# A chunk-attention and Fourier-mixing kernel: who issues the lower tiles' stores, and the order of the work around the first group's down projection

## The chip, the cores and the metric

The kernel runs on one core of one Trainium2 chip. The core has a matrix engine (TensorE, PE in the profile, with its weight loads shown as PEld), a vector engine (VectorE, DVE), a scalar engine (ScalarE, ACT), a general-purpose engine (GpSimd, POOL) and a sync engine (SyncE, SP) that only issues DMAs. Each engine has its own list of instructions and takes them in order; they meet through semaphores. The metric is the device time of one execution in microseconds (us).

## The reference

Eight batches of 576 tokens, 8 heads of 64. Attention runs within chunks of 64 tokens; the heads are joined to 512 features; then a Fourier mix and a two-layer network follow, with 2048 hidden features.

```python
scores = scale * np.matmul(q_c, k_c.transpose(0, 1, 2, 4, 3))      # chunks of 64
attn = softmax(scores)
x = (attn @ v_c) -> (B, S, H*D)
mixed = np.real(fft(fft(x, axis=1), axis=2))
u = x + mixed
un = (u - mean(u)) / sqrt(var(u) + 1e-6)
out = u + relu(un @ w_ch1) @ w_ch2
```

## The kernel before, in words

**Tiles and groups.** Tokens are taken in tiles of 128: per batch two *lower* tiles (`LO`, chunks from the front), two *higher* tiles (`HI`, chunks from the back, kept in mirrored order), and per pair of batches one *remainder* tile (`RE`). Group g of the two-layer network (g = 0 to 7) is the four tiles of batch g, in the order LO, HI, LO, HI; group 8 is the four remainder tiles. `first[b]` is the number of batch b's first tile; where b is even, that is its remainder tile.

**One main loop.** `mlp(g)` is a generator that emits the matrix work of group g: an up phase and a down phase. Each of its `yield`s is one step t of the main loop at the end of the kernel; in a step the loop emits, behind that matrix work, a share of everything else: the attention and Fourier work of the next batch (`side(b)`, a generator too), the rounding of weights, the sums and stores described below, and fetches. Nothing reorders this: what is emitted first stands first in its engine's list. Group 0's up phase is t = 1 to 16, its down phase (`down_plain`, L1236 and L1249) t = 17 to 32, where `begin[1]` = 32. `side(1)` is spread so that it ends at `ready_at[0]` = 25; its last three parts are the calls of `mixed` (L838 to L855), one for the remainder tile and two for the pairs of LO and HI tiles. They run the second Fourier product into a PSUM tile of tag `pt` (two buffers), copy half of it out on ACT (L843), join the halves on DVE (L848, L849), add them to the tile (on DVE for LO, on POOL for HI, L855) and take mean and variance (L702 to L707).

**Between two groups.** `normed(g, s)` normalises tile s (for g = 1 on ACT, L990 to L992), `turned(g, s)` transposes it on PE (L397) and copies it to `unT` (L1007). `combined(g, q)` makes sums of `unT`'s quarters on DVE (L1024 to L1028). Group 0's down phase calls `normed(1, j)` after block m = 9 + j and `turned(1, j)` after m = 11 + j, and `combined` right behind `turned` for j = 2 and 3.

**Fast products.** Groups 1 to 7 multiply with seven products in place of eight (`up_halves`, L1289; `down_halves`, L1341), which needs sums of the weights' quarters. For the first weight, `keep1(pair)` (four POOL instructions, L1069) makes three sums and overwrites one quarter, for one of four pairs of column blocks. Group 1 reads these sums in place; from group 2 on they, and the raw quarters, come back from a DRAM table `s1` through ten slabs (`fetch(1)`, L1155). `keep1_store` (L1074) writes the seven parts of each pair to `s1`, 256 KB each, 28 in all. For the second weight `keep2` (L1087, L1091) and `keep2_whole` (L1099) do the same into `s2`, read through three slabs of 1 MB (`fetch(2)`, L1160). `keep1(0)` is emitted at t = 31, pairs 1 to 3 at t = 33, 35, 37; the 28 stores two per step from t = 33. `conv2` runs the four `keep2` three parts per step, once all weights are rounded.

**Weights.** They arrive as 8-byte numbers, 512 KB a piece (L346), and are rounded to 4 bytes by a chain of DVE and ACT instructions (`round_weight`, L362 to L386).

**Stores of the result.** `store(n, o)` writes a finished tile: a lower tile as two DMAs of 64 rows in reversed order (L1037), both on SP; a higher tile as four DMAs, two on SP and two on ACT (L1046). SP also issues every load of q, k, v (L250, L273) and every fetch.

The lines in the loop that matter:

```python
ready_at = [begin[g] + (2 * KF - 7 if g < first_of[2] else 2 * HF + 4) for g in range(NG)]
conv2 = iter([step for i in range(HF // 2) for step in [keep2(i ^ 1)]])
...
if begin[1] - 1 <= t < begin[1] + 7 and t % 2:
    keep1((t - begin[1] + 1) // 2)
```

Of the kernel before, what the change touches and what calls it, by code (L numbers as in the profile page):

```python
# [16 lines left out]
def kernel(  # L17
# [32 lines left out]
    nc = tc.nc  # L50
# [350 lines left out]
    def att_T(n, which="qk"):  # L401

        if n > first[2]:
            for src, dst, nm in ((qs, qT, "qT"), (ks, kT, "kT")):
                if nm[0] not in which:
                    continue
                a = src.pop(n).rearrange("p j (t b d) -> p j t b d", t=4, b=2)[:, :, :, 0]  # L410
                t = one_p.tile([128, NJ, 2, CH + 1], FP32, tag=nm, name=nm)
                low = kind(n) == LO and nm == "qT"
                to = t[:, :, :, CH:0:-1] if low else t[:, :, :, 0:CH]
                if kind(n) == HI:
                    to = to[:, :, ::-1]
                nc.vector.transpose(out=to.rearrange("p j c (r t) -> p j t c r", t=4), in_=a)
                if low:
                    nc.gpsimd.tensor_copy(t[:, :, :, 0:1], t[:, :, :, CH:CH + 1])
                dst[n] = t.rearrange("p j c t -> p (j c) t")
            if n + 1 < NT:  # L420
                load(n + 1, which)
            return
        a = qs.pop(n)
        pt = turn(lambda j: a[:, 2 * j:2 * j + 2, :].rearrange("p h d -> p (h d)"))
        t = one_p.tile([128, 2 * NJ, CH + 1], FP32, tag="qT", name="qT")
        low = kind(n) == LO
        nc.scalar.copy(t[:, :, CH:0:-1] if low else t[:, :, 0:CH], pt.rearrange("p j (c t) -> p (j c) t", c=2))
        if low and n < first[1]:
            nc.scalar.copy(t[:, :, 0:1], t[:, :, CH:CH + 1])
        elif low:  # L430
            nc.gpsimd.tensor_copy(t[:, :, 0:1], t[:, :, CH:CH + 1])
        qT[n] = t
        a2 = ks.pop(n)
        pt = turn(lambda j: a2[:, 2 * j:2 * j + 2, :].rearrange("p h d -> p (h d)"))
        t = one_p.tile([128, NJ, 128], FP32, tag="kT", name="kT")
        nc.scalar.copy(t, pt)
        kT[n] = t.rearrange("p j (c t) -> p (j c) t", c=2)
        if first[1] <= n + 1 < NT:
            load(n + 1)
# [530 lines left out]
        yield  # L970


    uns, unTs = {}, {}

    def natural(n):

# [53 lines left out]
    def store(n, o):  # L1030

        last = n in groups[-1][1::2]
        for h, (b, c) in enumerate(chunks(n)):
            r0, t0 = h * CH, c * CH
            if kind(n) == LO:
                to = out[b, t0 + 1:t0 + CH + 1, :][::-1].rearrange("(i r) d -> r i d", r=2)[::-1]
                nc.sync.dma_start(out=to, in_=o[r0:r0 + CH])  # L1037
            elif kind(n) == RE:
                eng = nc.scalar if last and h else nc.sync
                eng.dma_start(out=out[b, t0 + 1:t0 + CH:2, :], in_=o[r0:r0 + ODD])  # L1040
# [27 lines left out]
        ):  # L1068
            nc.gpsimd.tensor_tensor(out=out_, in0=in0, in1=in1, op=op)  # L1069

    def keep1_store(i):
        pair, o = i // NO, (2, 1, 5, 3, 0, 4, 6)[i % NO]
        to = s1[pair, o].rearrange("p (k x) -> p k x", k=2)
        nc.sync.dma_start(out=to, in_=parts1(pair)[o])  # L1074

# [153 lines left out]
    def down_plain(g, h1):  # L1229
# [4 lines left out]
        for m in range(KF):  # L1234
# [14 lines left out]
                    nc.vector.tensor_tensor(out=o, in0=dn, in1=natural(n), op=ALU.add)  # L1249
                    store(n, o)  # L1250
            for j in range(G):
                due = KF - (G - j + 1)
                if m == due - 2:
                    normed(g + 1, j)
                if m == due:
                    turned(g + 1, j)
                    if j >= 2 and g + 1 >= first_of[1]:
                        combined(g + 1, j - 2)
            yield


# [175 lines left out]
    with tc.manual_schedule():  # L1437
# [60 lines left out]
        begin = [0]  # L1498
        for g in range(NG):
            begin.append(begin[-1] + (KF if g < first_of[1] else 2 * HF) + (KF if g < first_of[2] else 2 * NO if g < FEW else NR2 // 2))  # L1500
        ready_at = [begin[g] + (2 * KF - 7 if g < first_of[2] else 2 * HF + 4) for g in range(NG)]
        conv2 = iter([step for i in range(HF // 2) for step in [keep2(i ^ 1)]])

        def chain(gens):
            for gen in gens:
# [5 lines left out]
        for g in range(NG):  # L1511
            for _ in mlp(g):
# [7 lines left out]
                if cur < len(sides):  # L1520
                    t0 = 3 if cur == 0 else ready_at[cur - 1]
                    t1 = ready_at[cur]
                    due = min(sizes[cur], (t - t0) * sizes[cur] // (t1 - t0))
                    while done < due:
                        heavy = next(sides[cur], None) or heavy
                        done += 1
                    if t >= t1:
                        for _ in sides[cur]:
                            pass
                        cur, done = cur + 1, 0  # L1530
                if not heavy:
                    round_next(late if t < KF and t % 4 == 3 else None)
                    if t <= 2 or t < KF and t % 4 == 0 or t >= KF + 3:
                        round_next()
# [7 lines left out]
                if t == begin[1] - 1:  # L1542
                    for _ in conv2:
                        pass
                if begin[1] - 1 <= t < begin[1] + 7 and t % 2:
                    keep1((t - begin[1] + 1) // 2)
                if t == ready_at[NG - 3]:
                    rest_ = make_rest()
# [6 lines left out]
                    slab3.extend(a.rearrange("p (m e) -> p m e", m=4) for a in more)  # L1555
                if begin[FEW] + 2 <= t < begin[FEW] + 2 + NS3:
                    fetch(3)
                if begin[1] < t < begin[1] + KF:
                    for i in range(2):
                        if n_kept < HF // 2 * NO:  # L1560
                            keep1_store(n_kept)
                            n_kept += 1
                if t in (begin[1] + 9, begin[1] + 13, begin[1] + 16):
                    fetch(2)
                if t == begin[1] + KF:
# [51 lines left out]
```

## Time and profile before

| | |
|---|---|
| median of 3 runs | 1073.89 us (1072.86 to 1074.72) |
| the profiled execution | 1074.23 us, of which its span is 1072.2 us |
| TensorE busy | 1046.3 us (98%) |
| DVE, ACT, POOL busy | 610.8, 315.3, 406.6 us |
| DMA | 212.74 MB, mean 198 GB/s |
| TensorE clock | 1.00 throughout |

The span is the time from the first to the last record on the core; the rest of the execution lies around it. "Busy" counts computing instructions alone; issuing a DMA and waiting on a semaphore do not count. In a line of the time order the first number is the start in us from the beginning of the span, the second the duration of the group of instructions that the line merges, and a bracket gives how long the engine had been idle before and whose result ended that wait. `<-` reads "from": `h<-pa` is an instruction that writes `h` and reads `pa`. `L1289` is line 1289 of the kernel.

Group 0's up phase ends at about 115.6 us, its down phase at about 190.4 us; group 1 begins at 192.8 us.

### The profile page before, as it was taken

To read this page: it belongs to the slowest core of one execution; us is meant where nothing else is said; L and a number is where in the kernel's file an instruction comes from. 1 tells how busy PE (TensorE), PEld (TensorE's weight loads), DVE (VectorE), ACT (ScalarE), POOL (GpSimd) and SP (SyncE) were. 2 spreads that over 40 slices of the span, in tenths; PEclk is the share of its full clock that TensorE was granted. 3 is DMA by queue.
4 is the path that set the end of the run, shared out by engine and by line. 5 is a ranking of instruction groups with operands and counts; after the bars stand their busy time and mean duration, and the time that the engine had idled before them with its cause. 6 is when DMAs were issued, how large, how long until landed. Compare 5 with 4: busy or idle time off the path is not lost.

```text
span 1072.2 us, 20212 instructions
## 1 busy us (share of the span) xinstructions
PE 1046.3 (98%) x7498; PEld 854.6 (80%) x7498; DVE 610.8 (57%) x1319; ACT 315.3 (29%) x746; POOL 406.6 (38%) x531
## 2 busy tenths in 40 slices
PE   8999989899999999999999999999999999999997
PEld 6645444688888888888888888788888888888886
DVE  4798986684567465664565554745664535433331
ACT  4688563233113411322032312331133103101200
POOL 4310018672415140344134321614161726780281
PEclk9999999999999999999999999999999999999999
DMA  8767565489668546883667266954654559776763
GB/s 176 232 186 218 123 196 189 139 249 312 233 199 232 149 140 198 239 232 119 191 209 231 99 182 195 231 165 163 202 177 116 208 191 350 229 231 199 272 228 106
DMA packets 157759, 212.74 MB, mean 198 GB/s; under 512 B 69308, under 2 KB 103100, under 8 KB 151390
## 3 DMA queue, kind: packets, MB, share of 16 engines
q1 hardware_dynamic: 154012, 208.04, 63.4%
q10 hardware_dynamic: 3330, 2.76, 1.1%
q8 instruction: 60, 0.98, 0.4%
q0 software_dynamic: 320, 0.66, 0.3%
q14 instruction: 37, 0.30, 0.1%
HBM read 177.31 MB, written 34.08 MB: 197 GB/s over the span
## 4 chain that ended last, share of the span: by engine, by line
PE 77%; DVE 8%; DMA 5%; ACT 4%; SPq 3%; issue 2%; POOL 1%; DVEq 0%; ACTq 0%; POOLq 0%
PE pa L1289 19%; PE pb L1341 18%; PE pb L1289 14%; PE pa L1341 13%; PE dn L1405 4%; PE pt L397 2%; PE mix L838 2%; DMA xall<-in_moe_w_ch_dram 1%; SPq L263 1%; PE xp L498 1%; PE z L719 1%; DVE power L378 1%; DMA out_dram<-o 1%; PE sc L448 1%; DMA v<-in_v_dram 1%
## 5 line engine op out<-in xcount | busy, mean ns | idle before, releaser
L1289 PE MATMUL pa<-unT,wa 128*128 128x256 f32 x736 | 175.0, 381 | 2.5 <-DVE wa L1297 2.5
L1289 PEld LDWEIGHTS pa<-unT,wa 128*128 128x128 f32 x736 | 138.3, 190 | 21.8 <-DVE wa L1297 2.7
L1289 PE MATMUL pb<-wa 128*128 128x256 f32 x448 | 106.9, 381 | 0.1
L1341 PE MATMUL pa<-wb,h 128*128 128x256 f32 x448 | 101.5, 380 | 0.0
L1341 PE MATMUL pb<-wb,h 128*128 128x256 f32 x448 | 100.7, 379 | 0.0
L1289 PEld LDWEIGHTS pb<-wa 128*128 128x128 f32 x448 | 84.1, 190 | 12.3 <-DVE h L1299 0.5
L1341 PEld LDWEIGHTS pa<-wb,h 128*128 128x128 f32 x448 | 83.9, 190 | 11.3
L1341 PEld LDWEIGHTS pb<-wb,h 128*128 128x128 f32 x448 | 84.1, 190 | 11.0
L1169 POOL TENSOR_TENSOR h<-h 128x256 f32<-128x256 f32 x56 | 47.7, 860 | 102.3 <-DVE wb L1167 98.2
L555 POOL COPY xall<-xall 1x512 f32<-1x512 f32 x28 | 17.8, 636 | 154.3 <-DVE xall L515 126.9
L1295 DVE TENSOR_TENSOR wa<-pb,wa 128x256 f32<-128x256 f32 x56 | 23.8, 425 | 69.7 <-ACT wa L1294 69.7
L1289 PE MATMUL pb<-unT,wa 128*128 128x256 f32 x256 | 60.5, 379 | 0.0
L1303 ACT ACTIVATE h<-pa 128x256 f32<-128x256 f32 x64 | 24.6, 384 | 114.1 <-PE pa L1289 113.6
L1236 PE MATMUL dn<-wb,h 128*128 128x512 f32 x128 | 57.5, 597 | 0.0
L1294 ACT COPY wa<-pa 128x256 f32<-128x256 f32 x56 | 20.9, 372 | 123.5 <-PE pa L1289 80.6
L1289 PEld LDWEIGHTS pb<-unT,wa 128*128 128x128 f32 x256 | 48.6, 190 | 6.6
L1289 PE MATMUL pa<-wa 128*128 128x256 f32 x224 | 53.9, 383 | 0.0
L1309 ACT ACTIVATE h<-h 128x512 f32<-128x512 f32 x64 | 39.6, 629 | 45.0 <-DVE h L1308 44.8
L1341 PE MATMUL pb<-wb,yall 128*128 128x256 f32 x224 | 51.2, 381 | 0.0
L1341 PE MATMUL pa<-wb,yall 128*128 128x256 f32 x224 | 50.6, 379 | 0.3 <-DMA wb<-s 0.3
L1341 PE MATMUL pb<-wb 128*128 128x256 f32 x224 | 50.7, 379 | 0.0
L1195 PE MATMUL up<-unT,wa 128*128 128x512 f32 x108 | 49.4, 598 | 0.0
(299 smaller groups left out, 1976.1 us busy)
## 6 DMA issues: line engine op xcount, KB each, us to landing
wb<-s SPq DMA_DIRECT2D x49, 1024.0 KB
wa<-s SPq DMA_DIRECT2D x196, 256.0 KB
xall<-in_moe_w_ch_dram SPq DMA_DIRECT2D x22, 512.0 KB
q<-in_q_dram SPq DMA_DIRECT2D x96, 112.0 KB
k<-in_k_dram SPq DMA_DIRECT2D x96, 112.0 KB
wb<-s SPq DMA_DIRECT2D x16, 512.0 KB
v<-in_v_dram SPq DMA_DIRECT2D x124, 64.0 KB
s<-part SPq DMA_DIRECT2D x30, 256.0 KB
```

What stands on the lines that cost most here:

```text
L397: nc.tensor.transpose(pt[:, j, :], src(j), ident)
L838: nc.tensor.matmul(out=mix[:, cols], lhsT=zt[:, T], rhs=tab, start=(T == 0), stop=(T == 3), skip_group_check=True,)
L1169: nc.gpsimd.tensor_tensor(out=h1[:, m, hi], in0=h1[:, m, lo], in1=h1[:, m, hi], op=ALU.subtract)
L1195: nc.tensor.matmul(out=up, lhsT=w1[:, kk, m * 128:(m + 1) * 128], rhs=unT[:, kk], start=(kk == 0), stop=(kk == KD - 1), skip_group_check=True,
L1236: nc.tensor.matmul(out=dn, lhsT=h1[:, m, s * 128:(s + 1) * 128], rhs=w2[:, m, :], start=(m == 0), stop=(m == KF - 1),)
L1289: nc.tensor.matmul(out=dst, lhsT=w[:, kk, r], rhs=rhs[o][:, kk], start=(o in (0, 1) and kk == 0), stop=(kk == 1), skip_group_check=True,)
L1294: nc.scalar.copy(a, dst)
L1295: nc.vector.tensor_tensor(out=b, in0=pbs[r][:, 0], in1=a, op=ALU.add)
L1303: nc.scalar.activation(out=h1[:, m, lo], in_=dst, func=ACTF.Relu)
L1309: nc.scalar.activation(out=h1[:, HF + m], in_=h1[:, HF + m], func=ACTF.Relu)
L1341: nc.tensor.matmul(out=dst, lhsT=lhs[:, m], rhs=w[:, m], start=(o in (0, 2) and m == 0), stop=(m == HF - 1), skip_group_check=True,)
L1405: nc.tensor.matmul(out=dst, lhsT=lhs[:, m], rhs=w[:, m], start=(fresh and not half and m == 0), stop=(m == 3), skip_group_check=True,)
```

## The change

1. A lower tile's two stores are issued by GpSimd and no longer by SP.
2. Of the 28 stores of `s1`, the twelve of raw quarters (parts 0, 4 and 6 of each pair) are issued one per step at t = 17 to 20 and 24 to 31; the sixteen others one per step from t = 32.
3. `ready_at[0]` is 27 in place of 25. The last three parts of `side(1)` are spread over t = 25, 26 and 27. `side(2)` begins to count at 27.
4. `normed(1, j)` is called after blocks 10, 10, 12, 12 and `turned(1, j)` after blocks 12, 13, 14, 14.
5. `combined(1, 0)` and `combined(1, 1)` go into a list that the main loop empties behind that step's part of `side(2)`, which holds k's transpose.
6. `keep1(0)` runs between the second and the third `keep2` of `conv2`, and no longer at t = 31.
7. The copy of one column of a transposed lower q tile is named for ACT when the tile's number is `first[2]`.

```diff
-        if low and n < first[1]:
+        if low and (n < first[1] or n == first[2]):
             nc.scalar.copy(t[:, :, 0:1], t[:, :, CH:CH + 1])
...
             if kind(n) == LO:
                 to = out[b, t0 + 1:t0 + CH + 1, :][::-1].rearrange("(i r) d -> r i d", r=2)[::-1]
-                nc.sync.dma_start(out=to, in_=o[r0:r0 + CH])
+                nc.gpsimd.dma_start(out=to, in_=o[r0:r0 + CH])
...
-    def keep1_store(i):
-        pair, o = i // NO, (2, 1, 5, 3, 0, 4, 6)[i % NO]
+    def keep1_store(pair, o):
         to = s1[pair, o].rearrange("p (k x) -> p k x", k=2)
         nc.sync.dma_start(out=to, in_=parts1(pair)[o])
...
             for j in range(G):
-                due = KF - (G - j + 1)
-                if m == due - 2:
+                if m == (10, 10, 12, 12)[j]:
                     normed(g + 1, j)
-                if m == due:
+                if m == (12, 13, 14, 14)[j]:
                     turned(g + 1, j)
                     if j >= 2 and g + 1 >= first_of[1]:
-                        combined(g + 1, j - 2)
+                        joined.append((g + 1, j - 2))
...
-        ready_at = [begin[g] + (2 * KF - 7 if g < first_of[2] else 2 * HF + 4) for g in range(NG)]
-        conv2 = iter([step for i in range(HF // 2) for step in [keep2(i ^ 1)]])
+        ready_at = [begin[g] + (2 * KF - 5 if g < first_of[2] else 2 * HF + 4) for g in range(NG)]
+        late_due = {ready_at[0] - 4 + i: sizes[0] - x for i, x in enumerate((3, 3, 2, 1, 0))}
+
+        def first_sums():
+            keep1(0)
+            yield
+
+        conv2 = iter([keep2(1), keep2(0), first_sums(), keep2(3), keep2(2)])
...
                     due = min(sizes[cur], (t - t0) * sizes[cur] // (t1 - t0))
+                    if cur == 0:
+                        due = late_due.get(t, (t - t0) * sizes[cur] // (t1 - 2 - t0))
...
+                while joined:
+                    combined(*joined.pop(0))
                 if not heavy:
...
-                if begin[1] - 1 <= t < begin[1] + 7 and t % 2:
+                if begin[1] < t < begin[1] + 7 and t % 2:
                     keep1((t - begin[1] + 1) // 2)
...
-                if begin[1] < t < begin[1] + KF:
-                    for i in range(2):
-                        if n_kept < HF // 2 * NO:
-                            keep1_store(n_kept)
-                            n_kept += 1
+                if KF < t <= KF + 4 or KF + 8 <= t < KF + 16:
+                    keep1_store(n_kept // 3, (0, 4, 6)[n_kept % 3])
+                    n_kept += 1
+                if begin[1] <= t < begin[1] + KF:
+                    keep1_store((t - begin[1]) // 4, (2, 1, 3, 5)[(t - begin[1]) % 4])
```

More of the change, by code (lines that the diff above doesn't have):

```diff
@@ L970, in fourier_early @@
         yield
-    uns, unTs = {}, {}
+    uns, unTs, joined = {}, {}, []
     def natural(n):
```

## The prediction

> **What bounds the kernel now.** I read the head of the page first.
>
> ```profile
> span 1072.2 us, 20212 instructions
> PE 1046.3 (98%) x7498; PEld 854.6 (80%) x7498; DVE 610.8 (57%) x1319; ACT 315.3 (29%) x746; POOL 406.6 (38%) x531
> ```
>
> TensorE (PE) has work in 1046.3 of 1072.2 us. The change adds and removes no matmul, so all it can move is the 25.9 us in which PE stands still. The second view is who PE waits for (total, times, longest), the third PE's own instructions in order of time (start, duration, then in brackets the idle time before them), read for all brackets.
>
> ```profile
> PE pt L397 <- ACT un L992: 3.0, 3, 1.4
> PE pa L1289 <- DVE wa L1297: 2.5, 1, 2.5
> PE pb L1289 <- POOL wb L1069: 2.4, 1, 2.4
> PE mix L838 <- DVE y L849: 2.1, 1, 2.1
> ```
>
> ```profile
> 150.36 0.49 PE L838 MATMUL mix<-ce,zr 128*128 128x129 f32 x2 [1.84 <-ACT zr L785]
> 158.33 0.46 PE L838 MATMUL mix<-ce,zf 128*128 128x129 f32 x2 [2.06 <-DVE y L849]
> 172.21 0.65 PE L397 MATMUL pt<-ident,un 128*128 128x128 f32 x4 [1.42 <-ACT un L992]
> 181.72 0.62 PE L498 MATMUL xp<-v,pT 64*64 64x65 f32 x26 [0.41 <-ACT unT L1007]
> 192.78 1.99 PE L1289 MATMUL pb<-xall,wb 128*128 128x256 f32 x8 [2.41 <-POOL wb L1069]
> 212.28 0.70 PE L448 MATMUL sc<-kT,qT 64*64 64x64 f32 x32 [0.70 <-DVE kT L416]
> 673.19 1.99 PE L1289 MATMUL pa<-unT,wa 128*128 128x256 f32 x8 [2.49 <-DVE wa L1297]
> ```
>
> So the idle time is a short list. About 8 us lie before 110 us and about 5.4 us after the last matmul; the change touches neither. Between 140 and 193 us, the down phase of group 0 and its hand-over to group 1, there are five gaps, 8.14 us. Between 210 and 262 us there are four small ones (0.70, 0.26, 0.58, 0.25), 1.79 us. From 262 us to the end one gap matters, 2.49 us at 673. Ceiling of the gain: 12.4 us, 1061.8 us by the profiled execution's 1074.23 us (2.0 us lie around its span). The median of the three runs, 1073.89, is 0.34 lower; I work in differences and take them off the median.
>
> **What the skill says.** (1) The Trainium skill, "DMA: Bandwidth & Descriptors", section "Issuing engines are not separate DMA queues": moving a DMA to another issuing engine saves only the issue time. The trace has the price on both sides, 0.52 us for a lower tile's store on SP (median of 28), and for POOL (GpSimd):
>
> ```profile
> 1.47 5.64 POOL L273 DMA_DIRECT2D v<-in_v_dram  x9 [0.16 <-issue]
> ```
>
> that is 0.63 us each, though for loads of 64 KB. (2) Same page, "SWDGE vs HWDGE vs iDMA": a DMA engine serves GpSimd's queue and the hardware queues in turn, so POOL's stores leave the line in which SP's loads stand. No run here shows it yet. (3) "SBUF — State Buffer", "SBUF: two separate sides": VectorE with two SBUF inputs and GpSimd lock each other out, and GpSimd's descriptors can be held up by VectorE, 620 against 3100 ns. The first half agrees: the same token-sum instruction takes 1.37 us while POOL works and 0.42 us once POOL has ended at 186.2:
>
> ```profile
> 182.35 1.37 DVE L1025 TENSOR_TENSOR xall<-unT,xall 128x256 f32<-128x256 f32 x1
> 188.05 0.42 DVE L1025 TENSOR_TENSOR xall<-unT,xall 128x256 f32<-128x256 f32 x1
> ```
>
> The second half no run here shows.
>
> **The change, part by part.** Below, m counts the 3.46 us blocks of group 0's down projection; step t = 17 + m follows block m.
>
> *Transform tail spread.* Now `mixed` of the remainder comes after m=7, and both other `mixed` after m=8. The first waits 1.84 us for `zr`, the third 2.06 us for a PSUM tile that VectorE has not emptied. After: one each after m=8, 9, 10. `zr` was ready near 150.3; the first now starts at 144.82 + 2x3.46 = 151.7. The third comes 3.46 us after the second, near 161; its PSUM tile was freed at 158.2 and I expect 159.3, because the last weight's rounding now stands ahead of it on VectorE. Gain 3.9 us. The cover is one block, 3.46 us; without it both waits return.
>
> *Normalised tiles turned later.* `normed` moves to m=10,10,12,12, `turned` to 12,13,14,14. I follow ACT and VectorE: `mixed`(0) at 156.4, its two additions and statistics to 165.7, `un` of tiles 0 and 1 at 167.6 and 168.9; the first turn is due at 169.2. The 1.42 us goes, with 0.3 us to spare. `un` of tiles 2 and 3: 175.4 and 176.7, due 177.7. The 0.41 us goes too, since the step of the next batch that had it comes one block later; in its place the turn of `ex` needs a PSUM tile whose copy ends near 178.8: a new 0.4. Net 1.4.
>
> *First pair's weight sums ahead.* `keep1(0)`, four POOL instructions of 1.26 to 1.45 us, now begins at 190.1 and PE waits 2.41 us. In its new place behind two `keep2` it runs near 172 to 178; POOL's total stays. What is late next is VectorE's token sums: moved behind k's turn (1.1 us), they need the copies of tiles 2 and 3, both turned after m=14, the last copied near 180. Six instructions of 0.42 to 1.4 us make 2.5 to 8.4 us, then 0.62 us to empty the first PSUM tile. POOL still has `keep2` to near 188, so contention is likely. Group 1 can start between 184.9 (PE's own time) and 189; I take 186.1. Of the 2.41 us, 1.2 is gained; the ends are 2.4 gained and 1.8 lost.
>
> *Raw quarters stored sooner.* Twelve of 28 stores (256 KB each) leave the up phase of group 1 for t=17 to 20 and 24 to 31. SP is the crowded one in that up phase: the `wb<-s` fetch due near 238 went out at 254.8. Twelve issues of 0.55 us give SP 6.6 us back there, and the four small gaps, two of which trace to late k and slab loads, should shrink. On the other side the same 6.6 us come before 190, where SP mostly waits for roundings and POOL; DMA share there is 0.40 to 0.56 in five of seven stretches of 10 us (0.9 in 140 to 150 and 180 to 190). Weights are rounded five blocks ahead of use, so later loads cost nothing; without that lead each store would cost its 1.3 us (256 KB at 198 GB/s). The k load of step t=31 now stands behind the last `keep2` stores, which wait for POOL near 188; it is needed near 193. I take 0.6 gained, ends 1.8 gained and 2.5 lost.
>
> *Lower tiles' stores by GpSimd.* 32 stores of 128 KB go from SP to POOL, with their waits: each holds POOL until VectorE's last addition of that tile. Around 673 this is what SP and VectorE show:
>
> ```profile
> 649.78 5.84 SPq L1037 DMA_DIRECT2D out_dram<-wb  x2
> 657.13 3.59 SPq L273 DMA_DIRECT2D v<-in_v_dram  x4
> 662.40 4.77 SPq L250 DMA_DIRECT2D q<-in_q_dram  x4
> 671.80 1.09 DVE L416 STREAM_TRANSPOSE qT<-q 128x512 f32<-128x512 f32 x1 [4.12 <-DMA q<-in_q_dram]
> ```
>
> Two lower stores hold SP 5.84 us, v and q loads follow late, VectorE waits 4.12 us for q and PE 2.49 us behind it. Without the stores the q load goes out about 5 us sooner, more than the 4.12. Behind the stores on POOL stand the row shifts (L555) and the folds:
>
> ```profile
> 650.34 1.26 POOL L555 COPY xall<-xall 1x512 f32<-1x512 f32 x2 [10.79 <-DVE xall L515]
> 664.16 1.27 POOL L555 COPY xall<-xall 1x512 f32<-1x512 f32 x2 [12.55 <-DVE xall L515]
> ```
>
> They wait for VectorE 11 to 13 us anyway; 4 x 0.63 = 2.5 us per group is hidden there, and so would 4 x 3.1 be. I take 1.7: the 2.49 less 0.8 for a stall that the new order may open in another group; ends 2.5 gained and 1 lost.
>
> *First hunk.* It asks for a lower tile with number `first[2]`, but that tile is a remainder tile, so no instruction changes: zero.
>
> Sum: 3.9 + 1.4 + 1.2 + 0.6 + 1.7 = 8.8 us; 1073.89 - 8.8 = 1065.1.
>
> **Rivals.** *The waits come back in group 1.* PE arrives early and finds the token sums contended (1.8 lost), the k load late (2.5 lost), and 673 unchanged: 3.9 + 1.4 - 1.8 - 2.5 = 1.0 gained at worst, about 2.4 with half of the k loss: 1071.5. For it: POOL is busy throughout and VectorE strictly in order. Against: two ends of three terms at once.
>
> *Stores hidden anyway.* The 673 gap is chance; it stays or comes up in a neighbour, and SP's relief is worth nothing elsewhere, where PE has no gap to close: 8.8 - 1.7 = 7.1 gained, 1066.8.
>
> *Slower: POOL holds group after group.* If a store with its reversed rows and VectorE's lock held POOL not 0.63 but over 6 us, four of them would exceed the 23 us that POOL idles there per group. Folds and `added` would come late, and PE would wait in each of seven groups; 2 us each is 14 lost less 8.8: 1079. From 1.6 us a group it decides. For it: this use of POOL appears nowhere in this trace, with 128 KB and reversed rows. Against: the ten loads, and the idle time.
>
> **How the numbers follow.** Likeliest 0.57 (its own range 1062 to 1069), stores hidden 0.14, waits back 0.15, POOL slower 0.14. A measurement of this kernel tells about 0.2% (2.15 us) from no change. Faster takes the first two and half of the third: 0.78; within 0.2% the other half: 0.08; slower 0.14. The range 1062 (the ceiling) to 1073 takes in three cases and leaves out about 0.17.
>
> **What would show it.** The gaps before `mix` at L838 are gone from PE's list; so is the wait for POOL at L1069, with a wait for VectorE's sums at L1025 or L1249 of 0 to 4 us in its place. POOL shows 32 stores at L1037 near 0.6 us each; SP no longer has them. No gap near 665. From 262 us on, PE's idle is the tail alone. I am wrong if group 1 starts later than 190, if POOL's stores are over 3 us, or if gaps that recur with each group appear.

## The result, and the profile after

The changed kernel takes 1070.92 us (median of 20 runs, 1068.3 to 1074.7); beside it the kernel before took 1073.72 us (20 runs). The ratio is 0.9972, 95% interval 0.9963 to 0.9981: about 3.0 us faster. The forecast was 1065.1 us, 8.8 us faster. The sign was right, the size about three times too large.

The head of the changed kernel's page:

```profile
span 1067.8 us, 20222 instructions
PE 1046.2 (98%) x7498; PEld 855.4 (80%) x7498; DVE 610.7 (57%) x1319; ACT 315.3 (30%) x746; POOL 430.4 (40%) x563
```

TensorE's busy time is unchanged (1046.3 before), so the gain is again standing time. Whom TensorE waits for (total, times, longest):

```profile
PE sc L448 <- POOL qT L418: 2.9, 1, 2.9
...
PE mix L838 <- DVE y L849: 1.4, 1, 1.4
PE pa L1287 <- ACT xall L1292: 1.3, 1, 1.3
...
PE sc L448 <- DVE kT L416: 0.9, 1, 0.9
```

Of the four waits shown of before, those for `un`, for `wa` and for `wb` at L1069 have shrunk or gone, and `mix` keeps 1.4 of 2.1 us. At the top stands a new one: TensorE waits 2.9 us for GpSimd (POOL), but for a copy of one column of a transposed q tile (L418), not for weight sums. TensorE's own instructions in order of time (start, duration, idle before in brackets):

```profile
162.93 0.46 PE L838 MATMUL mix<-ce,zf 128*128 128x129 f32 x2 [1.37 <-DVE y L849]
...
189.16 1.04 PE L448 MATMUL sc<-kT,qT 64*64 64x64 f32 x32 [2.88 <-POOL qT L418]
190.13 3.27 PE L1287 MATMUL pb<-xall,wb 128*128 128x256 f32 x8
...
196.38 1.99 PE L1287 MATMUL pa<-xall,wb 128*128 128x256 f32 x8 [1.26 <-ACT xall L1292]
...
205.53 0.70 PE L448 MATMUL sc<-kT,qT 64*64 64x64 f32 x32 [0.91 <-DVE kT L416]
```

Group 1 begins at 190.13 us; before it was 192.78. But the first block of group 1 takes 3.27 us where it took 1.99: TensorE runs it at half clock behind the 2.88 us gap (the last section). The old gap near 673 us is gone.

The balance of the two profiled executions, whose spans differ by 4.4 us: between 140 and 193 us the gaps fall from 8.14 to 4.84 us, +3.3; the half clock takes back about 1.7; between 193 and 262 us the gaps grow from 1.79 to 2.32 us, -0.5; 673 us gives +2.5. That makes 3.6; the rest of 0.8 I could not place. The two profiled executions stand further apart than the medians do, and over all runs the mean clock of both kernels is alike (0.997), so the half clock belongs to this pair of traces more than to the 3.0 us.

Why GpSimd is late is in its own list:

```profile
175.40 1.27 POOL L1069 TENSOR_TENSOR wb<-wa 128x512 f32<-128x512 f32 x1
...
187.44 1.32 POOL L1086 TENSOR_TENSOR yall<-wb,yall 128x512 f32<-128x512 f32 x1
188.71 0.40 POOL L418 COPY qT<-qT 128x8 f32<-128x8 f32 x1
189.06 1.27 POOL L1086 TENSOR_TENSOR yall<-wb 128x512 f32<-128x512 f32 x1
```

The four sums of the first pair (L1069) now run from 175.40 to 180.5 us, and the `keep2` sums behind them stand about 5 us later: the last runs to 191.6 us where it ended at 186.2. The column copy, done at 178.4 us before, is done at 189.1. Two parts of the change add up there: with items 3 to 5 alone it starts at 183.8 us in place of 178.2, and the four sums ahead push it on to 188.7. VectorE (DVE) works beside GpSimd all that time. Its token sums:

```profile
182.04 1.38 DVE L1025 TENSOR_TENSOR xall<-unT,xall 128x256 f32<-128x256 f32 x1
...
186.27 1.37 DVE L1025 TENSOR_TENSOR xall<-unT,xall 128x256 f32<-128x256 f32 x1
```

Before, the second of these took 0.42 us, since GpSimd had ended; now both are long, and the six sums fill 181.5 to 189.0 us.

The stores did what was asked. SP has none of L1037 any more; around 660 us its loads of v, q and k follow each other, and on GpSimd a store costs 0.68 us (28 of them, mean 677 ns in the page's groups), the pair of one tile 1.32 us:

```profile
653.97 2.64 SPq L273 DMA_DIRECT2D v<-in_v_dram  x4
656.70 1.03 SPq L1154 DMA_DIRECT2D wa<-s  x2
657.82 2.50 SPq L250 DMA_DIRECT2D q<-in_q_dram  x4
```

```profile
644.68 1.32 POOL L1037 DMA_DIRECT2D out_dram<-wb  x2 [6.14 <-DVE wb L1359]
```

### The profile page after: what moved, and what is told of

Same layout as the page of the kernel before. It is cut to its first block, busy times and chain, and to the rows that moved or that the text cites. A ratio compares the mean times of both kernels' runs of the same rounds, so it can differ in the third digit from the quotient of the medians.

```text
span 1067.8 us, 20222 instructions
## 1 busy us (share of the span) xinstructions
PE 1046.2 (98%) x7498; PEld 855.4 (80%) x7498; DVE 610.7 (57%) x1319; ACT 315.3 (30%) x746; POOL 430.4 (40%) x563
## 4 chain that ended last, share of the span: by engine, by line
PE 83%; DVE 4%; DMA 4%; ACT 3%; POOL 3%; SPq 2%; issue 1%; ACTq 0%; POOLq 0%; DVEq 0%
PE pa L1287 20%; PE pb L1339 18%; PE pb L1287 15%; PE pa L1339 14%; PE dn L1403 4%; PE pt L397 2%; DMA xall<-in_moe_w_ch_dram 2%; PE up L1194 2%; PE mix L838 2%; PE xp L498 2%; PE z L719 1%; POOL wb L1069 1%; SPq L263 1%; PE sc L448 1%; DMA s<-yall 1%
## 5 line engine op out<-in xcount | busy, mean ns | idle before, releaser
L1037 POOL DMA_DIRECT2D out_dram<-wb x28 | 18.9, 677 | 117.8 <-DVE wb L1356 81.8
```

## The experiments

Items are numbered as in the list of the change: 1 stores by GpSimd, 2 raw quarters stored sooner, 3 tail spread, 4 later turns, 5 token sums behind k's turn, 6 first pair's weight sums ahead. Ratios are to the kernel before, run beside each on the same chip (its median there between 1073.2 and 1074.4 us).

### First: the new wait, and the stores

**The column copy on ScalarE** (changed kernel; the engine of the copy at L418 is another for one tile).

```diff
-                    nc.gpsimd.tensor_copy(t[:, :, :, 0:1], t[:, :, :, CH:CH + 1])
+                    (nc.scalar.copy if n == first[2] + 1 else nc.gpsimd.tensor_copy)(t[:, :, :, 0:1], t[:, :, :, CH:CH + 1])
```

> The changed kernel, with the one-column copy of the transposed q tile number first[2]+1 issued by ACT in place of POOL. Theory A (the copy is the wait): the 2.88 us gap of TensorE before the scores at 189 us and the 3.4 us at half clock that follow it (1.7 us) go; about 1066.3 us, 4.6 less than the changed kernel. Theory B (the token sums bind right behind it): the six sums on VectorE still end near 189, group 1 starts at most 0.6 us sooner; TensorE's gap stays, now as a wait for VectorE; about 1070.3 us.

Measured 1071.31 us, ratio 0.9972 (0.9965 to 0.998): no change from the changed kernel, theory B. The wait for GpSimd is gone and one of 3.00 us for VectorE stands in its place:

```profile
189.78 1.97 PE L1287 MATMUL pb<-xall,wb 128*128 128x256 f32 x8 [3.00 <-DVE o L1248]
```

So the copy was only the last of two waits that end half a microsecond apart; behind it stand VectorE's token sums and the first output after them (L1248). The copy that item 7 names is another one (L429): both traces have two of these on ScalarE, so item 7 did nothing, as predicted.

**Both removed** (the copy on ScalarE, and eight of `keep2`'s sixteen GpSimd sums left out).

```diff
-            nc.gpsimd.tensor_tensor(out=out_, in0=in0, in1=in1, op=op)
+            if i < 2:
+                nc.gpsimd.tensor_tensor(out=out_, in0=in0, in1=in1, op=op)
```

> The kernel of the first run here (copy on ACT), and the eight POOL sums of the last two keep2 left out, so the second weight's table is not right for half of its rows. Theory A (the copy was the wait): nothing further is won, 1066.3 us as in the first run. Theory B (VectorE's token sums bind, slowed by POOL): the six sums take 2.6 us in place of 7.5, group 1 starts 3 to 4.5 us sooner than in the first run, and the time is 1065.5 to 1067 us while the first run is near 1070.

Measured 1061.53 us, 0.9889 (0.9874 to 0.9904), faster than either theory. With GpSimd out of the way every token sum is short:

```profile
180.08 0.42 DVE L1025 TENSOR_TENSOR xall<-unT,xall 128x256 f32<-128x256 f32 x1
```

So 9.4 us of the changed kernel hang on these eight sums: the long token sums, the stores of `s2` that wait for them, the loads behind those stores, and the half clock that gaps bring. TensorE's gaps between 140 and 262 us are down from 7.16 to 1.71 us, and the time is that of the prediction's ceiling (1061.8 us). The kernel leaves needed work out, so it shows what hangs on these sums and is no way to get there.

**Stores back on SP** (changed kernel without item 1).

```diff
-                nc.gpsimd.dma_start(out=to, in_=o[r0:r0 + CH])
+                nc.sync.dma_start(out=to, in_=o[r0:r0 + CH])
```

> The changed kernel, with the lower tiles' stores issued by SP again. Theory A (the stores on SP made the gap at 673 us): a gap of 2 to 2.5 us comes back somewhere between 262 us and the end, and the time is 1073 to 1073.5 us. Theory B (that gap was chance of the one order of loads): no gap from 262 us on, 1070.5 to 1071.5 us.

Measured 1077.41 us, 1.003 (1.0018 to 1.0041): slower than before, and than both theories. Without item 1 the change would have lost. A gap near 673 us came back, as theory A says, but a longer one, which neither names, stands at 215.8 us. TensorE, and VectorE at the same place:

```profile
215.83 3.70 PE L1287 MATMUL pb<-unT,wa 128*128 128x256 f32 x8 [5.83 <-DVE xall L1293]
...
675.00 2.00 PE L1287 MATMUL pa<-unT,wa 128*128 128x256 f32 x8 [1.73 <-DVE wa L1295]
```

```profile
214.34 1.09 DVE L416 STREAM_TRANSPOSE qT<-q 128x512 f32<-128x512 f32 x1 [9.04 <-DMA q<-in_q_dram]
```

The q load goes out at 210.62 us, behind four lower stores, four higher stores, a v load and two stores of `s1` on SP; VectorE waits 9.04 us for it, TensorE 5.83 us for VectorE.

**Stores alone** (the kernel before with item 1).

```diff
-                nc.sync.dma_start(out=to, in_=o[r0:r0 + CH])
+                nc.gpsimd.dma_start(out=to, in_=o[r0:r0 + CH])
```

> The kernel before, with only the lower tiles' stores moved to POOL. Theory A (the stores on SP made the gap at 673 us): that gap is gone, 1071.2 us, 2.5 less than before. Theory B (POOL pays for it): POOL's sums for group 1, which stand behind the stores, come later and the start of group 1 loses what is won; 1073.7 us or more.

Measured 1071.32 us, 0.9975 (0.9965 to 0.9985): 2.7 us gained, theory A. The gap at 673 us left TensorE's list, and with it the two small ones before the scores at 212 us and for the slab at 261 us (0.70 and 0.25 us). The 1.42 us before the turn of `un` are missing too, but only because TensorE came later to it, at half clock behind an earlier gap. In all traces with the lower stores on SP, TensorE waits 1.2 to 2.6 us in all behind 262 us; in none with item 1 does it wait more than 0.5.

Item 1 is worth 2.7 us on the kernel before and about 6.2 us inside the change (0.9972 against 1.003); the trace above shows where the rest comes from, SP's crowd before 216 us.

### Second: can the waits be taken away one by one?

**Token sums from PSUM.** The sums stand right behind the turns and read two inputs from the PSUM tile of the turn; the column copy is on ScalarE.

```diff
+        p12, p22 = (pts[g, 2 + q_][:, 0:2], pts[g, 2 + q_][:, 2:4]) if g == 1 else (b12, b22)
-        nc.vector.tensor_tensor(out=t1, in0=b12, in1=b11, op=ALU.subtract)
+        nc.vector.tensor_tensor(out=t1, in0=p12, in1=b11, op=ALU.subtract)
...
-                        joined.append((g + 1, j - 2))
+                        combined(g + 1, j - 2)
```

> The changed kernel with the column copy on ACT, and the token sums for group 1 called right behind the turns of tiles 2 and 3, with one operand each read from the PSUM tile and not from SBUF, so that POOL cannot lock them out; all of POOL's work stays. Theory A (the sums' lock is what holds group 1): six sums in 2.6 to 4 us in place of 7.5, group 1 starts near 186 in place of 189.8, and the time falls by 4 us to about 1067. Theory B (the k load is next): TensorE arrives earlier at the scores of the second lower tile and waits there for k not 3.35 but 6 to 7 us, since k stands on SP behind the last keep2 stores; about 1070.5.

Measured 1071.46 us, 0.9977 (0.9967 to 0.9987): nothing gained, though each sum now takes 0.42 us while GpSimd works, and the last ends at 184.3 us, 4.7 us sooner:

```profile
182.46 0.42 DVE L1027 TENSOR_TENSOR xall<-pt,xall 128x256 f32<-128x256 f32 x1
```

```profile
182.15 1.27 POOL L1088 TENSOR_TENSOR xall<-wb,xall 128x512 f32<-128x512 f32 x1
```

TensorE waits for ScalarE (ACT) instead, a wait that neither theory has, and ScalarE's list shows why: four store issues hold it 5.43 us, against 2.42 us before.

```profile
196.65 3.37 PE L1289 MATMUL pa<-xall,wb 128*128 128x256 f32 x8 [4.48 <-ACT xall L1294]
```

```profile
190.75 5.43 ACTq L1048 DMA_DIRECT2D out_dram<-o  x4
```

**The same, with `keep2`'s last stores two steps later.**

```diff
-                    for _ in range(3):
+                    for _ in range(2 if t == begin[1] - 2 else 0 if t == begin[1] - 1 else 3):
-                if t == begin[1] - 1:
+                if t == begin[1]:
```

> The kernel of the run before, and the stores of the last keep2 called two steps later, behind the k load. Theory A (the sums alone): nothing further, 1067. Theory B (the k load is next): the wait for k falls to under 1 us; about 1065 to 1066, the best of all correct kernels here.

Measured 1070.26 us, 0.9968 (0.9955 to 0.9981). The k wait, only 0.23 us in the run before, went; ScalarE's remains (3.08 us). Both theories had 1067 us or less.

**Then ScalarE's store issues to GpSimd.**

```diff
-                    eng = nc.scalar if r else nc.sync
+                    eng = (nc.gpsimd if n < first[1] else nc.scalar) if r else nc.sync
```

> The run before last in the chain (column copy on ACT, sums from PSUM, last keep2 stores two steps later), and of group 0's higher tiles the half of the stores that ACT issues is issued by POOL. Theory A (ACT is held 5 to 6 us by issuing four stores in a full DMA queue, and TensorE waits for its first copy): the gap of 3.1 to 4.5 us at the third product of group 1 and the half-clock stretch behind it go, 1066 to 1067 us. Theory B (that wait hides another behind it): TensorE waits as long for VectorE or for k, 1070 us.

Measured 1071.45 us, 0.9979 (0.997 to 0.9989). Theory B: ScalarE's wait is gone, and one of 4.09 us for VectorE, which waits 7.23 us for a q load, has come:

```profile
212.57 2.96 PE L1289 MATMUL pb<-unT,wa 128*128 128x256 f32 x8 [4.09 <-DVE xall L1295]
```

**And the raw quarters in their old place** (item 2 undone on top of that).

```diff
-                if KF < t <= KF + 4 or KF + 8 <= t < KF + 16:
...
+                if begin[1] < t < begin[1] + KF:
```

> The kernel of the run before, with the raw quarters' stores in their old place. Theory A (early raw stores fill the queue just when group 1 starts): 1 us less than the run before, near 1065.5. Theory B (they relieve the up phase of group 1): 1 to 2 us more, with a gap near 260 us for a slab.

Measured 1068.29 us, 0.9946 (0.9934 to 0.9958): 2.8 us under the changed kernel by the ratios, with 4.21 us still waited at 210.9 us.

The first three of these kernels are within 1.2 us of each other, and none is clear of the changed kernel: as one wait is removed, the next late thing of the same crowd takes its place. The fourth is another matter. It and the run before it were measured side by side, and undoing item 2 gained 3.5 us (0.9979 to 0.9946, the intervals apart): here the early raw stores cost something, though the largest wait stayed. In the traces 1.20 us of it is the wait of the third `mix`, which is gone, and the mean clock rose from 0.996 to 0.998; the division was not settled.

### Third: the parts of the change, apart

**Order alone** (the kernel before with items 3, 4 and 5).

```diff
-                if m == due - 2:
+                if m == (10, 10, 12, 12)[j]:
...
-                if m == due:
+                if m == (12, 13, 14, 14)[j]:
...
-                        combined(g + 1, j - 2)
+                        joined.append((g + 1, j - 2))
...
-        ready_at = [begin[g] + (2 * KF - 7 if g < first_of[2] else 2 * HF + 4) for g in range(NG)]
+        ready_at = [begin[g] + (2 * KF - 5 if g < first_of[2] else 2 * HF + 4) for g in range(NG)]
...
```

> The kernel before with only the order of the vector work changed: tail spread, later normed and turned, token sums behind k's turn; stores, weight sums and raw quarters as before. Theory A (the waits in the tail were worth their length, 5.3 us): 1068.5. Theory B (TensorE only comes earlier to a start of group 1 that POOL and the token sums hold until 188 to 189, and k's load is late after it): 1071 to 1073.

Measured 1069.82 us, 0.9966 (0.9954 to 0.9979): 3.7 us gained, between the theories. The third `mix` still waits 1.29 us, and group 1 waits for the first pair's sums as it did before:

```profile
188.50 1.99 PE L1288 MATMUL pb<-xall,wb 128*128 128x256 f32 x8 [2.42 <-POOL wb L1069]
```

**Stores and order** (the kernel before with items 1, 3, 4 and 5): the diff just shown, and

```diff
-                nc.sync.dma_start(out=to, in_=o[r0:r0 + CH])
+                nc.gpsimd.dma_start(out=to, in_=o[r0:r0 + CH])
```

> The kernel before with the lower tiles' stores on POOL and the order of the vector work changed; weight sums and raw quarters as before. Alone the first gave 2.6 us, the second 3.8. Theory A (the parts add up, and what the changed kernel lacks is lost by the two others): 1067.3. Theory B (both draw on the same gap at 673 us and POOL's stores push the weight sums of pairs 0 and 1 back): 1069.5 to 1071.

Measured 1066.12 us, 0.9937 (0.992 to 0.9954): 6.8 us gained (the interval is 4.9 to 8.6), theory A: the 2.7 and 3.7 us of the two alone add up as far as can be told. Leaving items 2 and 6 out makes the changed kernel faster by about 3.8 us (0.9972 to 0.9937).

**First sums alone** (the kernel before with item 6).

```diff
-        conv2 = iter([step for i in range(HF // 2) for step in [keep2(i ^ 1)]])
+        conv2 = iter([keep2(1), keep2(0), first_sums(), keep2(3), keep2(2)])
...
-                if begin[1] - 1 <= t < begin[1] + 7 and t % 2:
+                if begin[1] < t < begin[1] + 7 and t % 2:
```

> The kernel before with only the first pair's weight sums moved between the second and third keep2. Theory A (the 2.41 us wait for POOL at the start of group 1 was worth its length): 1071.3. Theory B (the sums and column copy behind it come later by those four POOL instructions, 5 us, and the last keep2 stores and k's load with them): 1073.5 or more.

Measured 1076.24 us, 1.0029 (1.002 to 1.0038): 3.1 us lost, theory B. The wait of 2.41 us for `wb` became one of 3.05 us for VectorE, and VectorE's second set of token sums, 0.42 us each before, is long:

```profile
193.79 3.04 PE L1289 MATMUL pb<-xall,wb 128*128 128x256 f32 x8 [3.05 <-DVE o L1249]
```

```profile
189.42 1.37 DVE L1025 TENSOR_TENSOR xall<-unT,xall 128x256 f32<-128x256 f32 x1
```

**First sums back** (the changed kernel with item 6 undone).

```diff
-        conv2 = iter([keep2(1), keep2(0), first_sums(), keep2(3), keep2(2)])
+        conv2 = iter([step for i in range(HF // 2) for step in [keep2(i ^ 1)]])
...
-                if begin[1] < t < begin[1] + 7 and t % 2:
+                if begin[1] - 1 <= t < begin[1] + 7 and t % 2:
```

> The changed kernel with one part undone: the first pair's weight sums (keep1(0)) are emitted at t = 31 again. Everything else of the change stays: stores by GpSimd, tail spread, turns and token sums later, raw quarters stored sooner. Before ran 1073.9, the changed kernel 1070.9, the kernel with stores and order alone 1066.1 us. Theory A: the early sums carry the whole 4.8 us between the last two (alone they lost 3.1 us); with them back the time is 1066 to 1067.5 us, and group 1 begins near 187.7 us with a wait of about 2.4 us for POOL's wb. Theory B: the early raw stores carry a good part of it, as SP is behind before group 1; then 1068.5 to 1070 us, with SP's q and k loads for batch 2 late and a wait for kT or the token sums between 195 and 216 us.

Measured 1066.78 us, 0.9933 (0.9914 to 0.9952): theory A. Undoing item 6 gains 0.0039 of the time, 4.2 us. TensorE again waits 2.41 us for `wb`, but starts group 1 at 188.70 us, 1.43 us sooner than the changed kernel, at full clock (1.99 us for the first block):

```profile
188.70 1.99 PE L1287 MATMUL pb<-xall,wb 128*128 128x256 f32 x8 [2.41 <-POOL wb L1069]
...
209.40 1.97 PE L1287 MATMUL pb<-unT,wa 128*128 128x256 f32 x8 [1.00 <-DVE xall L1293]
```

The column copy is issued at 184.0 us there, 4.7 us sooner, and TensorE does not wait for it.

**Raw stores late** (the changed kernel with item 2 undone).

```diff
-                if KF < t <= KF + 4 or KF + 8 <= t < KF + 16:
-                    keep1_store(n_kept // 3, (0, 4, 6)[n_kept % 3])
...
+                if begin[1] < t < begin[1] + KF:
+                    for i in range(2):
...
```

> The changed kernel with all 28 stores of the first weight's table in their old place, two per step from t = 33. Theory A (their earlier place relieves SP): the small gaps of the up phase of group 1 come back, 1072 to 1072.5. Theory B (earlier, they only crowd SP and the DMA engines where k's load and ACT's stores are issued): 1070 or less, with the gap before k's scores smaller than 0.9.

Measured 1069.83 us, 0.9974 (0.996 to 0.9989), against 0.9972 with item 2: no difference that can be told. The same without item 6: 0.9937 without item 2, 0.9933 with it. In these two pairs item 2 is worth nothing that can be told. In the chain above it cost 3.5 us; in no pair here does it gain.

**Raw stores alone** (the kernel before with item 2).

```diff
-                if begin[1] < t < begin[1] + KF:
...
+                if KF < t <= KF + 4 or KF + 8 <= t < KF + 16:
+                    keep1_store(n_kept // 3, (0, 4, 6)[n_kept % 3])
```

> The kernel before with one part of the change: the twelve raw quarters are stored at t = 17 to 20 and 24 to 31, the sixteen others one a step from t = 32. Theory A: the relief of SP in group 1's up phase is worth its 6.6 us of issue time in part, and the gaps at 212 to 262 us shrink: 1072 to 1073 us. Theory B: the stores push the loads that stand behind them on SP before 190 us, and cost as much or more than they give back: 1073.7 to 1075.5 us, with longer waits of VectorE for k or q between 195 and 216 us.

Measured 1080.01 us, 1.0051 (1.0033 to 1.0069): 5.5 us lost, more than theory B allowed. TensorE, VectorE and SP at the places that differ:

```profile
151.59 0.49 PE L838 MATMUL mix<-ce,zr 128*128 128x129 f32 x2 [3.21 <-ACT zr L785]
...
219.25 1.14 PE L448 MATMUL sc<-kT,qT 64*64 64x64 f32 x32 [4.78 <-DVE kT L416]
```

```profile
144.47 0.43 DVE L370 TENSOR_SCALAR power<-xall 128x512 uint32<-128x512 uint32 x1 [1.04 <-DMA xall<-in_moe_w_ch_dram]
...
218.11 1.09 DVE L416 STREAM_TRANSPOSE kT<-k 128x512 f32<-128x512 f32 x1 [7.82 <-DMA k<-in_k_dram]
```

```profile
210.41 3.16 SPq L250 DMA_DIRECT2D k<-in_k_dram  x4
```

The k load goes out at 210.41 us; it was 202.15. And `zr` is ready 1.2 us later than before (the wait was 1.84 us): raw stores on SP push the weights' loads, VectorE waits 0.46, 0.99 and 1.04 us for the last three of them ahead of the transform, where it waited 0, 0.47 and 0.59, and the transform's work stands behind these roundings on VectorE and ScalarE. In this trace TensorE's clock also halves behind three gaps, for 13.7 us together (the last section); over all its runs the mean clock is 0.994, beside 0.995 for the kernel before, so this is a part of the 5.5 us at most. How the 5.5 us divide between waits and clock was not settled.

**Raw stores and stores by GpSimd** (the kernel before with items 1 and 2): the diff just shown, and

```diff
-                nc.sync.dma_start(out=to, in_=o[r0:r0 + CH])
+                nc.gpsimd.dma_start(out=to, in_=o[r0:r0 + CH])
```

> The kernel before with two parts: raw quarters stored sooner and the lower tiles' stores by GpSimd. Raw quarters alone ran 1080.0, stores by GpSimd alone 1071.3, before 1073.9 us. Theory A: the loss of the raw stores has two places, zr later by 1.2 us at 151 us (weights' loads behind the stores on SP, so rounding late, so ACT late), and the k load behind SP's other stores (4.78 us of wait at 219 us in place of 0.70); with the lower stores off SP the second goes and the first stays: 1071.5 to 1073.5 us, with a wait of about 3.2 us before mix and below 1.5 us for kT. Theory B: the loss is that of DMA traffic and does not depend on SP's queue: near 1077 us, the sum of both alone.

Measured 1072.25 us, 0.9992 (0.9986 to 0.9999): theory A. With the lower stores off SP the k wait is back to 0.78 us:

```profile
214.15 0.69 PE L448 MATMUL sc<-kT,qT 64*64 64x64 f32 x32 [0.78 <-DVE kT L416]
```

So most of item 2's loss alone is SP's queue, which item 1 relieves: on top of item 2, item 1 gains 6.3 us, as much as inside the change, and 2.7 us without it. Against stores alone (0.9975) item 2 still costs 1.8 us, with 2.35 us waited for `zr` and 2.25 for `un`. With items 3 to 5 as well nothing that can be told is left of it (sums back against stores and order); that items 3 and 4 put one more block ahead of those waits fits this, but no run tests it by itself.

### Fourth: a version that beats both

**Stores and order, token sums from PSUM** (items 1, 3, 4, and the sums as in the first of the second set; against the run of stores and order).

```diff
+        p12, p22 = (pts[g, 2 + q_][:, 0:2], pts[g, 2 + q_][:, 2:4]) if g == 1 else (b12, b22)
-        nc.vector.tensor_tensor(out=t1, in0=b12, in1=b11, op=ALU.subtract)
+        nc.vector.tensor_tensor(out=t1, in0=p12, in1=b11, op=ALU.subtract)
...
-                        joined.append((g + 1, j - 2))
+                        combined(g + 1, j - 2)
```

> Stores by GpSimd and the order of the work (1066.1 us so far), and now the token sums of group 1 stand right behind the turns and read two of their inputs from PSUM, so that they take the short form of about 0.42 us. Theory A: VectorE's token sums are what group 1 waits for next in that kernel too; 1064 to 1065.2 us. Theory B: POOL's sums of the first pair of weights, which end near 187.6 us, set group 1's start in that kernel, and shorter token sums change nothing or cost the 1.8 us that the turn of ex then waits for the sums: 1066 to 1068 us, with TensorE's wait for POOL's wb (L1069) still there.

Measured 1064.01 us (1062.93 to 1064.34), 0.9903 (0.9883 to 0.9922): 10.4 us under the kernel before. TensorE:

```profile
181.63 0.63 PE L397 MATMUL pt<-ident,ex 128*128 128x128 f32 x4 [1.69 <-DVE unT L1028]
187.05 1.99 PE L1290 MATMUL pb<-xall,wb 128*128 128x256 f32 x8 [0.26 <-POOL wb L1071]
...
255.09 3.69 PE L1342 MATMUL pa<-wb,yall 128*128 128x256 f32 x16 [2.00 <-DMA wb<-s]
```

Theory A by time. The 1.69 us that theory B named are there, and the wait for `wb` has shrunk to 0.26 us, mostly because TensorE now comes 1.6 us later to it: group 1 begins at 187.05 us, only 0.6 us sooner than with stores and order, but at full clock, where that trace ran the first block at half clock. Against stores and order the gain is 2.1 us by the medians and 3.7 us by the ratios, and the two intervals just meet, so it is likely and not certain. On the changed kernel the short sums were worth nothing: there ScalarE and q stood behind them.

**The same with item 2.**

```diff
-                if begin[1] < t < begin[1] + KF:
...
+                if KF < t <= KF + 4 or KF + 8 <= t < KF + 16:
+                    keep1_store(n_kept // 3, (0, 4, 6)[n_kept % 3])
```

> The changed kernel with the first pair's weight sums at t = 31 again, and the token sums of group 1 right behind the turns, read from PSUM: the 1064.0 us kernel plus the raw quarters stored sooner. That kernel's last idle stretch of size is 2.00 us at 255 us, where TensorE waits for a slab load (wb from s) that SP issues late. Theory A: the sooner stores relieve SP in that up phase, the slab wait goes and nothing new comes: 1062 to 1063 us. Theory B: the sooner stores take as much elsewhere (k or q loads behind them, or weights): 1064 to 1066 us.

Measured 1065.64 us (1064.36 to 1066.55), 0.9922 (0.9908 to 0.9936): theory B. The slab wait of 2.00 us went, and 0.97 us before `mix` and 0.60 us at 208 us came. The interval meets that of the run without item 2; item 2 gains nothing here, and whether it loses stays open.

## Why the prediction was right or wrong

**First pair's weight sums ahead** is the step that failed: +1.2 in the sum, -4.2 us measured inside the change (-3.1 alone), outside its own end of -1.8. That is 5.4 of the 5.8 us by which the forecast missed. Three things in it were wrong. First, "POOL's total stays" is true and beside the point: the four sums went ahead of eight `keep2` sums, a column copy and the last `s2` stores, and all of these became about 5 us later. I followed the sums' effect on VectorE only, and did not list what was queued behind them on GpSimd; the copy at L418 is in no line of my working, and TensorE waited 2.88 us for it, though without it the token sums hold group 1 nearly as long. Second, I saw that "contention is likely" and put it into the range of the start (184.9 to 189), but took 186.1; with GpSimd busy to 191.6 us the long form, 8.4 us for six, was the one to take, and they took 7.5. The Trainium skill's "SBUF — State Buffer", section "SBUF: two separate sides", describes the shared lock, and the runs agree with it: 1.37 us with GpSimd at work, 0.42 with it gone, and 0.42 beside a working GpSimd where the two inputs came from PSUM and SBUF. Third, I treated the 2.41 us wait for `wb` as a thing to be taken away, when the move only changed it for another: before, GpSimd stood idle from 186.2 us on, so VectorE's second three token sums were short and done at 188.8 us, before TensorE needed them. With the sums moved ahead and nothing else, GpSimd worked through that time, these three took 4.2 us in place of 1.2, and TensorE waited 3.05 us for VectorE. My sign of error, "group 1 starts later than 190", came true by 0.13 us.

**Transform tail spread** and **Normalised tiles turned later**: 5.3 us in the sum, 3.7 measured (interval 2.3 to 4.9). The waits for `zr` and `un` went as worked out. The third `mix` kept 1.29 us with these items alone and 1.37 in the changed kernel: its PSUM tile, which I expected free at 159.3 us, was free at 162.8, behind VectorE's rounding. Two instructions of that rounding took 1.75 us each where others of the kind take 0.68; both ran beside GpSimd's sums.

**Lower tiles' stores by GpSimd**: +1.7 in the sum, 2.7 measured alone and 6.2 inside the change. The place (673 us) and the price (0.63, measured 0.68 us) held. The term was small because I costed only one gap: the same stores stand ahead of the q and k loads at the start of group 1, where the other items made SP late. The Trainium skill's statement in "DMA: Bandwidth & Descriptors", section "Issuing engines are not separate DMA queues", that another issuing engine saves the issue time alone, fits a store by itself; in a list in strict order the relief was the whole time the stores stood ahead of the loads, 5.84 us at one place before.

**Raw quarters stored sooner**: +0.6 in the sum; inside the change nothing that can be told, -1.8 us beside item 1, and -5.5 us alone. "Weights are rounded five blocks ahead of use, so later loads cost nothing" looked at the weights' users only; the rounding itself stands ahead of the Fourier work on VectorE and ScalarE, and VectorE was already waiting for the loads. Item 1 relieves the late k load and items 3 to 5 seem to cover the rest; the step names none of them.

**The rivals.** *The waits come back in group 1* was nearest, 1071.5 us against 1070.92, with the token sums contended as it said. That its number fits is partly luck: the late k load was small (0.91 us) and the 673 gap did close, while the contended sums cost more than its 1.8 us. *Stores hidden anyway* is excluded by the runs with stores alone and with the stores back on SP. *POOL holds group after group* is excluded: 0.68 us a store, no gap that recurs with each group.

The sum of the measured parts, 2.7 + 3.7 + 0 - 4.2 = 2.2 us, agrees with the 3.0 us of the whole within what the intervals allow (1 to 2 us each).

## What to carry to other kernels

When a step is moved ahead on an engine that works in order, list everything that it now stands in front of, down to the smallest copy, and follow each to the engine that waits for it; that the engine's total stays the same says nothing. Where several waits end within a microsecond of each other, as the column copy and the token sums do here, the one that the profile names is worth only its lead over the next, so cost an edit by the second-latest arrival. And parts of a change can hide each other's cost: the early raw stores lose 5.5 us alone and nothing that can be told where other parts cover them, so each part needs a run of its own before it is kept.

## What the runs showed of the hardware that was not expected

**Half clock after a short gap.** Behind, or late in, some gaps of 2.1 to 5.8 us TensorE falls to half clock for about 3.4 us (or twice that) by the trace's clock record; 3.4 us at half clock are 1.7 us of work not done. Windows of the changed kernel and of the one with stores and order (the columns: window, its length, busy time of each engine with instructions, granted TensorE clock, DMA share, GB/s):

```profile
190.00:192.00 2.00, 2.00 (x13) 1.52 (x7) 1.93 (x7) 0.00 (x0) 2.00 (x3) 0.50 0.98 350
```

```profile
188.00:191.00 3.00, 3.00 (x9) 2.37 (x8) 2.90 (x9) 0.00 (x0) 3.00 (x4) 0.51 0.46 129
```

```profile
187.65 3.41 PE L1288 MATMUL pb<-xall,wb 128*128 128x256 f32 x8 [2.42 <-POOL wb L1069]
```

```profile
192.66 3.21 PE L1289 MATMUL pb<-xall,wb 128*128 128x256 f32 x8 [2.40 <-POOL wb L1069]
```

The last two lines are the block behind the gap in the second of these kernels and in the one with stores alone. In the kernel before, the same block took 1.99 us behind a gap of 2.41 us. The kernel with stores alone and the kernel before are nearly alike at this place: TensorE was busy 1.1 of the 3.5 us up to the block in both. So at this length the half clock comes in some executions and not in others, and what decides it was not found. The Trainium skill, "TensorE: Matmul & The Clock Gate", section "HAM oscillation — how this bites in real kernels", gives "no PE-idle gaps >~3.4µs" as the rule; here gaps of 2.4 us were enough. A gap of this size can so cost up to 1.7 us more than its length, a term that the prediction did not have.

Over 128 runs of the kernel before the price is milder: the 37 with a mean clock of 0.999 or more took 1073.4 us on average, the 12 of 0.994 or less, which is at least 10 us more at half clock, 1075.6. With few gaps the mean clock is higher (0.998 and 0.999 in the two kernels of the fourth set), with long ones lower (0.9945 with the stores back on SP). A part of the differences between the runs above is therefore clock and not standing time, and was not separated.

**ScalarE held by its own stores.** Issuing four 64 KB stores held ScalarE 2.42 us before, with the DMA engines busy 0.55 of that time, and 5.43 us with token sums from PSUM, where they were busy 0.92 of it. That the crowd of transfers is the cause is likely from this, but was not taken apart.
